# Third product of mixer 1 as a fourth inner seven-product, joined operand sums, and fillers spread over four inner products

## The chip, the cores and the metric

The kernel runs on one core of one Trainium2 chip. The metric is the time of one execution on the device in microseconds (us). The 35 executions of the kernel before agree within 0.2% (566.54 to 567.64 us), and kernels are compared only with the runs of the kernel before that were taken on the same chip in the same call, several rounds each. The results also list the mean clock that TensorE was granted in each run, with 1.0 as full speed.

Five engines appear below. TensorE (PE) multiplies matrices, and its weight loads (PEld) overlap the multiplications (in the kernel before they are busy 296.6 us and the multiplications 558.1, in a span of 566.0). VectorE (DVE) adds and subtracts. ScalarE (ACT) copies and applies gelu. SP and GpSimd play no part in the argument.

## The reference

The reference is one block of linear attention followed by a "mixer" MLP that works across the sequence. Only the first product of the mixer matters here.

```python
x = A_x                                             # 1 x 2048 x 1024, bf16
h = x + _A_ref(_layernorm(x, axis=-1), A_wqkv, A_wo)    # _A_ref is cut: linear attention, 32 heads
# _B_ref(_layernorm(h), w1, b1, w2, b2):
h = _layernorm(x, axis=-1)
u = jnp.einsum("bsd,sf->bdf", h, w1) + b1           # w1: 2048 x 3584: "mixer 1"
u = _gelu(u)
y = jnp.einsum("bdf,fs->bds", u, w2) + b2           # w2: 3584 x 2048: "mixer 2"
# cut: the result is h before the second layernorm, plus y transposed
```

## The kernel before

The kernel computes mixer 1 with a product of 2x2 blocks that needs seven multiplications instead of eight (of the Strassen-Winograd kind). A `Product7` object is one row block of the result. Its seven products are `p1` to `p7`; the products 5, 6, 7 and 3 need a left operand that is a sum of blocks, made by `asum` on VectorE. Two such objects make a `Quad`. Mixer 1 is seven quads: quad 0 is special, and quads 1 to 6 ("steady quads") all run through `run1`.

Inside a quad, some products of the two row blocks together are done once more by a seven-product, an `Inner`. It replaces 2 x 8 matmuls of 512 columns by 7 x 4 matmuls of 256 columns, and it pays with sums on VectorE and copies on ScalarE. The kernel before does this for product 1 (`in1`), product 5 (`in5`) and product 2 (`in2`). Product 3 is still sixteen plain matmuls (`sts[0].p3()`, `sts[1].p3_mm()`).

```python
class Inner:
    # ... (cut: __init__)
    def sums(self):                       # four operand sums on VectorE
        sm = [pools["is"].tile([P, self.nk, P], FP16, tag=self.tag, bufs=pools["is_bufs"], name="is")[:] for _ in range(4)]
        dve.tensor_tensor(sm[0], self.a21, self.a22, ALU.add)
        dve.tensor_tensor(sm[1], sm[0], self.a11, ALU.subtract)
        dve.tensor_tensor(sm[2], self.a11, self.a21, ALU.subtract)
        dve.tensor_tensor(sm[3], self.a12, sm[1], ALU.subtract)
        self.lhs.update({5: sm[0], 6: sm[1], 7: sm[2], 3: sm[3]})
    # ... (cut: mm, four matmuls of 256 columns)
    def i1(self):
        # ... (cut: takes the PSUM banks a, b, c, e)
        self.mm(1, self.a, True)
        nc.scalar.copy(self.b, self.a)    # L254: product 6 adds into this copy
    def i6(self):
        self.mm(6, self.b, False)
        nc.scalar.copy(self.c, self.b)    # L258
    # ... (cut: i2, i5)
    def i7(self):
        self.mm(7, self.c, False)
        self.sink_sum(1, 1, self.c, self.es[:])
    def i3(self):
        self.mm(3, self.b, False)
        self.sink_sum(0, 1, self.b, self.es[:])
    def i4(self):
        self.mm(4, self.c, False)
        self.sink(1, 0, self.c)           # what takes the result out of the bank
```

The steps of an inner product depend on each other through copies and adds. `interleave` therefore puts "fillers" between them, matmuls of 512 columns of other products that TensorE can do meanwhile. The names in quotation marks are points at which other work is put into the program.

```python
def interleave(self, n, fs, at={}):
    steps = [(f, k) for f in fs for k in range(self.sts[0].nk)]
    t = len(steps)
    cuts = [0, (5 * t + 8) // 16, (9 * t + 8) // 16, (12 * t + 8) // 16, t]
    # ... (cut)
    for f in (
        n.i1, "in", 0, n.i6, n.i2, 1, n.i5, n.i7, flush, 2, "mid", n.i3, "third", 3, n.i4, "out", flush,
    ):      # 0 to 3: the next share of the fillers
        # ... (cut)

def sink1(self, m, h, ps):                # result of in1: into A, and a copy into B
    A, B, c = self.sts[m].A, self.sts[m].B, self.cols(h)
    nc.scalar.copy(A[:, c], ps)
    nc.scalar.copy(B[:, c], A[:, c])

def sum1(self, m, h, ps, es):             # the same where a sum is due
    A, B, c = self.sts[m].A, self.sts[m].B, self.cols(h)
    dve.tensor_tensor(A[:, c], ps, es, ALU.add)
    nc.scalar.copy(B[:, c], A[:, c])

def run1(self, pend, nxt, on_p4):
    sts = self.sts
    def starting():
        self.asums(5)
        self.in5 = Inner(sts, 5, self.mov5, "i5", self.sink5, self.sum5)
        self.in5.sums()
        pend[1].p3_evac()
        for st in sts:
            st.begin(based=True)

    self.interleave(
        self.in1, [st.p4 for st in pend], {"in": starting, "mid": partial(sts[0].asum, 6)}
    )
    sts[1].asum(6)
    self.asums(7)
    in2 = Inner2(sts, 2, self.mov2, "i1", self.sink2, None)
    in2.sums()
    # ... (cut)
    self.interleave(self.in5, [st.p6 for st in sts])
    sts[0].finish()
    self.asums(3)
    self.interleave(in2, [st.p7_fill for st in sts], {
        "third": lambda: sts[0].evac(0, 0, sts[0].A), "out": lambda: sts[1].evac(0, 0, sts[1].A),
    })
    if nxt is not None:
        nxt.begin1()
    sts[0].p3()
    sts[1].p3_mm()
    return sts, nxt
```

Matmuls and the VectorE work of `dve` are pinned in mixer 1: they run in the order of the program.

## Time and profile before

| | kernel before |
|---|---|
| median of 3 runs | 566.69 us (566.56 to 567.57) |
| span of the profiled run | 566.0 us |
| PE / DVE / ACT busy | 99% / 73% / 49% |
| granted clock | 1.0 |
| the six steady quads | 23.22 us the first, then 22.98 or 22.99 |

The page of the profile starts with the busy time of each engine. Further down stands the chain of work that ended last, by engine; "issue" is time in which the engine waited for nothing that the profile shows, and a q behind a name (below, SPq) is the engine's sequencer. These lines are from the page of the kernel before.

```profile
span 566.0 us, 8365 instructions
...
PE 558.1 (99%) x3127; PEld 296.6 (52%) x3143; DVE 411.3 (73%) x798; ACT 277.4 (49%) x585; POOL 1.8 (0%) x8
...
PE 96%; DVE 2%; ACT 1%; issue 1%; DMA 0%
```

TensorE is busy almost all the time, and the granted clock of this run is 1.0. So a change gains where it takes matmul time away without opening a gap, and VectorE has time to spare only as long as its results come when TensorE asks for them.

The next view is the table of stretches for the first and the third steady quad of the kernel before, one quad to a row. In the kernel before the rows start 0.60 us behind the first matmul of the quad's first inner product (255.79 and 302.00), where the modelled end of product 1 stands. After the length come the busy time and the number of instructions of each engine, the granted clock, and the transfers.

```profile
core 0: us, PE busy (x) PEld busy (x) DVE busy (x) ACT busy (x) POOL busy (x), PEclk, DMA share, GB/s
256.39:279.61 23.22, 23.21 (x149) 14.46 (x148) 18.20 (x40) 11.77 (x26) 0.00 (x0) 1.00 0.29 92
302.60:325.58 22.98, 22.98 (x149) 14.48 (x148) 16.22 (x37) 11.75 (x26) 0.00 (x0) 1.00 0.30 93
```

The third quad has 22.98 us of PE work in 22.98 us. VectorE works 16.2 us in a quad and ScalarE 11.75.

The place is the start of the second inner product, `in5`. Here is TensorE's order in time, from the kernel before. The columns are start and length in us, then engine, line and operation, the output and the inputs with their sizes, and a count of equal instructions in a row.

```profile
308.51 0.60 PE L216 MATMUL psI<-hE,sa 128*128 128x256 f16 x4
308.94 1.24 PE L216 MATMUL psB<-hT,sa 128*128 128x512 f16 x5
310.02 0.60 PE L216 MATMUL psI<-hi,is 128*128 128x256 f16 x4
```

Product 1 of `in5` starts at 308.51, five fillers at 308.94, product 6 at 310.02. Five fillers at 0.2158 us each end exactly at 310.02, so there is no gap. The lengths shown overlap: each 512-column matmul is listed with 0.379 us although the next starts after 0.2158. (The notes of the profile page call the ends of matmuls modelled.) I therefore measure gaps between start times: a gap is the next start minus the last start minus the issue spacing.

Product 6 needs ScalarE's copy of product 1. This is ScalarE in order of time at the same place; a bracket gives the idle time before an instruction and what ended it.

```profile
308.38 0.38 ACT L495 COPY psB<-a 128x256 f32<-128x256 f32 x1 [0.61 <-DVE a L216]
308.70 0.68 ACT L419 ACTIVATE gO<-psC,b_sb 128x512 f16<-128x512 f32 x1
309.28 0.36 ACT L489 COPY a<-psI 128x256 f32<-128x256 f32 x1
309.53 0.39 ACT L254 COPY psI<-psI 128x256 f32<-128x256 f32 x1
```

The copy at line 254 is the one. It starts at 309.53 and ends at 309.92, 0.10 us before product 6. Before it ScalarE does a copy that waits for a VectorE add, a gelu, and a copy out of PSUM. They ran in that order: the copy starts at 308.38, after 0.61 us in which ScalarE idled for the add, and the gelu behind it at 308.70, although the last matmuls into the `psC` that it reads are listed from 307.21 to 308.24.

### The profile page before, as it was taken

To read this page: it belongs to the slowest core of one execution; us is meant where nothing else is said; L and a number is where in the kernel's file an instruction comes from. 1 tells how busy PE (TensorE), PEld (TensorE's weight loads), DVE (VectorE), ACT (ScalarE), POOL (GpSimd) and SP (SyncE) were. 2 spreads that over 40 slices of the span, in tenths; PEclk is the share of its full clock that TensorE was granted. 3 is DMA by queue.
4 is the path that set the end of the run, shared out by engine and by line. 5 is a ranking of instruction groups with operands and counts; after the bars stand their busy time and mean duration, and the time that the engine had idled before them with its cause. 6 is when DMAs were issued, how large, how long until landed. Compare 5 with 4: busy or idle time off the path is not lost.

```text
span 566.0 us, 8365 instructions
## 1 busy us (share of the span) xinstructions
PE 558.1 (99%) x3127; PEld 296.6 (52%) x3143; DVE 411.3 (73%) x798; ACT 277.4 (49%) x585; POOL 1.8 (0%) x8
## 2 busy tenths in 40 slices
PE   7999999999999999999999999999999999999997
PEld 3444444454444444456666666665445655645643
DVE  6898888544776788878768676676979749658725
ACT  4647777766766877645446454464210311311211
POOL 1000000000000000000000000000000000000000
PEclk9999999999999999999999999999999999999999
DMA  9933342115764751104041340422983922912111
GB/s 300 295 75 75 75 89 43 19 39 200 217 198 137 254 185 74 74 1 129 23 148 35 116 148 2 149 78 53 242 222 95 264 71 75 293 43 75 38 47 46
DMA packets 86088, 67.13 MB, mean 119 GB/s; under 512 B 15762, under 2 KB 80032, under 8 KB 86048
## 3 DMA queue, kind: packets, MB, share of 16 engines
q1 hardware_dynamic: 85312, 65.94, 40.6%
q10 hardware_dynamic: 672, 0.66, 0.3%
q8 instruction: 24, 0.39, 0.3%
q14 instruction: 16, 0.13, 0.1%
q0 software_dynamic: 64, 0.01, 0.0%
HBM read 54.54 MB, written 8.91 MB: 112 GB/s over the span
## 4 chain that ended last, share of the span: by engine, by line
PE 96%; DVE 2%; ACT 1%; issue 1%; DMA 0%
PE acc_t L216 18%; PE psI L216 16%; PE psC L216 15%; PE psB L216 15%; PE psA L216 4%; PE psC L814 4%; PE psB L814 4%; PE psA L814 4%; PE acc_t L738 3%; PE psA L325 2%; PE psB L325 2%; PE acc_t L1089 2%; PE psE L814 2%; PE psC L325 2%; PE kvps L767 1%; PE psE L325 1%
## 5 line engine op out<-in xcount | busy, mean ns | idle before, releaser
L216 PEld LDWEIGHTS <-sa 128*128 128x128 f16 x651 | 63.7, 98 | 48.5 <-issue 0.2
L216 PEld LDWEIGHTS <-wq 128*128 128x128 bf16 (+1 forms) x629 | 61.1, 98 | 46.8
L216 PEld LDWEIGHTS <-is 128*128 128x128 f16 x472 | 46.1, 98 | 21.6 <-DVE hi L216 0.4
L216 PE MATMUL acc_t<-wo_sb,pqT 128*128 128x512 f16 x256 | 55.6, 379 | 0.0
L216 PE MATMUL psC<-gs,wq 128*128 128x512 f16 (+2 forms) x210 | 45.0, 365 | 0.0
L216 PE MATMUL acc_t<-xnT,wq_sb 128*128 128x512 bf16 x188 | 43.1, 379 | 0.2
L216 PEld LDWEIGHTS <-pqT 128*128 128x128 bf16 x256 | 25.0, 98 | 30.5 <-issue 0.6
L178 DVE TENSOR_SCALAR e_sb<-e_sb 128x512 bf16<-128x512 bf16 x64 | 18.6, 290 | 27.9 <-ACT e_sb L174 27.3
L174 ACT ACTIVATE e_sb<-acc_t 128x512 bf16<-128x512 f32 x40 | 23.9, 597 | 24.6 <-PE acc_t L216 12.0
L814 PEld LDWEIGHTS <-xs 128*128 128x128 f16 x208 | 20.0, 98 | 23.4 <-DVE xs L800 1.3
L216 DVE TENSOR_TENSOR ot<-ot,hr 128x512 bf16<-128x512 bf16 (+2 forms) x27 | 11.2, 414 | 28.1 <-ACT ot L466 27.7
L216 PEld LDWEIGHTS <-wq_sb 128*128 128x128 bf16 x192 | 18.5, 98 | 23.0 <-issue 1.3
L362 ACT COPY psC<-psB 128x512 f32<-128x512 f32 x22 | 12.5, 570 | 34.6 <-PE psB L216 29.9
L216 PE MATMUL psB<-hT,sa 128*128 128x512 f16 x112 | 28.7, 379 | 0.0
L216 PE MATMUL psC<-hT,sa 128*128 128x512 f16 x112 | 28.3, 379 | 0.0
L216 DVE BATCH_NORM_STATS2 hst<-acc_t 128x6 f32<-128x512 f32 x32 | 21.4, 692 | 9.1 <-ACT h_bf L216 8.9
L216 DVE TENSOR_TENSOR a<-psI,a 128x256 f32<-128x256 f32 x36 | 14.7, 422 | 17.9 <-PE psI L216 17.2
L254 ACT COPY psI<-psI 128x256 f32<-128x256 f32 x25 | 9.1, 364 | 37.7 <-PE psI L216 37.4
L814 PE MATMUL psA<-wkv,xnT 128*128 128x512 bf16 x98 | 26.0, 379 | 0.3
L216 PE MATMUL psB<-hO,sa 128*128 128x512 f16 x112 | 25.3, 379 | 0.0
L814 PEld LDWEIGHTS <-xnT 128*128 128x128 bf16 x156 | 15.2, 98 | 18.5 <-issue 0.2
L258 ACT COPY psI<-psI 128x256 f32<-128x256 f32 x25 | 8.9, 357 | 32.3 <-PE psI L216 32.3
(202 smaller groups left out, 1046.2 us busy)
## 6 DMA issues: line engine op xcount, KB each, us to landing
wq<-in_B_w_dram SPq DMA_DIRECT2D x14, 1024.0 KB, 7.9
wq<-in_B_w_dram SPq DMA_DIRECT2D x8, 1792.0 KB, 9.2
xr<-in_A_x_dram SPq DMA_DIRECT2D x16, 256.0 KB, 4.7
rdb<-rd_dram SPq DMA_DIRECT2D x32, 128.0 KB, 4.0
h_dram<-h_bf SPq DMA_DIRECT2D x16, 256.0 KB, 2.0
hr<-h_dram SPq DMA_DIRECT2D x32, 128.0 KB, 2.6
out_dram<-ot SPq DMA_DIRECT2D x31, 128.0 KB, 1.7
x_sb<-in_A_x_dram SPq DMA_DIRECT2D x15, 256.0 KB, 3.0
```

Of the source, the lines that this page charges most:

```text
L174: pin(nc.scalar.activation(e_sb[:], src, ACT.Exp))
L178: pin(nc.vector.tensor_scalar(e_sb[:], e_sb[:], 1.0, PHI_EPS, ALU.min, ALU.add))
L216: return (lambda *a, **kw: pin(op(*a, **kw))) if self.always or Held.on else op
L254: nc.scalar.copy(self.b, self.a)
L258: nc.scalar.copy(self.c, self.b)
L325: pe.matmul(ps[:, cols], lhsT=lhs[:, k, :], rhs=mv(k)[:, cols], start=(start and k == 0), stop=(k == self.nk - 1), skip_group_check=True,)
L362: nc.scalar.copy(self.C[:], self.B[:])
L738: mm = nc.tensor.matmul(pp[:, 0:CW], lhsT=xnT[:, kt, i * P:(i + 1) * P], rhs=wkv[:, kt, c * CW:(c + 1) * CW], start=(kt == 0), stop=(kt == ...
L767: pin(nc.tensor.matmul(kv_ps[b][:, sl, :], lhsT=pks[i % NPK][:, j * P:(j + 1) * P], rhs=vaugs[i % NVA][:, j, :], start=False, stop=(i == N ...
L814: pin(nc.tensor.matmul(ps[:], lhsT=lhs[:, k, :], rhs=rhs[:, k, :], start=(start and k == 0), stop=(k == hk2 - 1), skip_group_check=True,))
L1089: nc.tensor.matmul(qp[:, 0:SW], lhsT=wq_sb[:, kt, j * P:(j + 1) * P], rhs=xnT[:, kt, u * SW:(u + 1) * SW], start=(kt == 0), stop=(kt == ND ...
```

## The change

The change has four parts.

1. Product 3 becomes a fourth inner seven-product, `in3`. That is 28 matmuls of 256 columns instead of 16 of 512. Its moving operand, the right half of `hO` (the last quarter of `h`), needs four 1024-wide sums (`sums3`, into the tile `hi`), once, in the first steady quad.
2. The operand sums of the two row blocks are made in one instruction of twice the width.
3. The fillers are spread over four inner products: 16, 12, 12 and 8 matmuls instead of 16, 16 and 16.
4. The sums of an inner product may be made in two parts, so that they can be placed separately.

The core of the diff, with cuts marked:

```diff
@@ Inner
-        def sums(self):
-            # ... four instructions
+        def sums(self, part=slice(0, 4)):
+            # ... the same four instructions, those in `part`
@@ Quad
         def asums(self, m):
-            for st in self.sts:
-                st.asum(m)
+            # ... (cut: Mixer2 as before; a, b are now views over both row blocks)
+            t = self.S[m] = pools["sa"].tile([P, NSP, 2, P], FP16, tag="sa", name="sa")[:]
+            for s, st in enumerate(self.sts):
+                st.lhs[m] = t[:, :, s, :]
+            return dve.tensor_tensor(t, a, b, op)
@@ run1
-        def run1(self, pend, nxt, on_p4):
+        def run1(self, pend, nxt, on_p4, before_third=nop):
             sts = self.sts
+            s4, s6, s7 = self.steps(*[st.p4 for st in pend]), self.steps(*[st.p6 for st in sts]), self.steps(*[st.p7_fill for st in sts])
+            c6, c7 = 3 * len(s6) // 4, len(s7) // 2
             def starting():
+                self.in1.sums(slice(2, 4))
                 self.asums(5)
                 self.in5 = Inner(sts, 5, self.mov5, "i5", self.sink5, self.sum5)
-                self.in5.sums()
-                pend[1].p3_evac()
-                # ...
+                self.in5.sums(slice(0, 2))
+                self.asums(6)
+                # ...
-            self.interleave(
-                self.in1, [st.p4 for st in pend], {"in": starting, "mid": partial(sts[0].asum, 6)}
-            )
-            sts[1].asum(6)
+            self.interleave(self.in1, s4, {"in": starting, "mid": lambda: self.in5.sums(slice(2, 4))})
             self.asums(7)
             # ...
-            self.interleave(self.in5, [st.p6 for st in sts])
+            self.interleave(self.in5, s6[:c6])
             sts[0].finish()
             self.asums(3)
-            self.interleave(in2, [st.p7_fill for st in sts], {
+            self.base3()
+            in3 = Inner2(sts, 3, self.mov3, "i5", self.add_to(self.t3), None)
+            in3.sums()
+            before_third()
+            sts[0].with_shared(sts[0].base3, sts[0].B)
+            self.interleave(in2, s6[c6:] + s7[:c7], {
                 # ...
-            sts[0].p3()
-            sts[1].p3_mm()
+            self.interleave(in3, s7[c7:], {
+                "third": lambda: sts[0].evac(0, 1, sts[0].base3), "out": lambda: sts[1].evac(0, 1, sts[1].base3),
+            })
@@ main
+    mov3, sums3 = inner_moving(hO[:, :, CW:D], NSP, inner1, "hi3")
-        pend, nxt = cur.run1(pend, lambda: ..., next_load1(u + 1))
+        pend, nxt = cur.run1(pend, lambda: ..., next_load1(u + 1), sums3 if u == 1 else nop)
```

The result of product 5 in `Inner2` is added to both row blocks by one broadcast instruction, and intermediate sums are written in place.

More of the change, by code (lines that the diff above doesn't have):

```diff
@@ L2 @@
 from functools import partial
+from itertools import groupby
 import concourse.bass as bass
@@ L229, in __init__ @@
             self.lhs = {1: self.a11, 2: self.a12, 4: self.a22}
-        def sums(self):
-            sm = [pools["is"].tile([P, self.nk, P], FP16, tag=self.tag, bufs=pools["is_bufs"], name="is")[:] for _ in range(4)]
-            dve.tensor_tensor(sm[0], self.a21, self.a22, ALU.add)
-            dve.tensor_tensor(sm[1], sm[0], self.a11, ALU.subtract)
-            dve.tensor_tensor(sm[2], self.a11, self.a21, ALU.subtract)
-            dve.tensor_tensor(sm[3], self.a12, sm[1], ALU.subtract)
-            self.lhs.update({5: sm[0], 6: sm[1], 7: sm[2], 3: sm[3]})
+        def sums(self, part=slice(0, 4)):
+            if part.start == 0:
+                self.sm = [pools[self.tag].tile([P, self.nk, P], FP16, tag=self.tag, bufs=pools["is_bufs"], name="is")[:] for _ in range(4)]
+                self.lhs.update(zip((5, 6, 7, 3), self.sm))
+            sm = self.sm
+            for o, a, b, op in (
+                (sm[0], self.a21, self.a22, ALU.add), (sm[1], sm[0], self.a11, ALU.subtract),
+                (sm[2], self.a11, self.a21, ALU.subtract), (sm[3], self.a12, sm[1], ALU.subtract),
+            )[part]:
+                dve.tensor_tensor(o, a, b, op)
         def mm(self, m, ps, start):
@@ L283, in i5 @@
             self.mm(5, self.e, True)
-            for m in range(2):
-                self.sink(m, 1, self.e)
+            self.sink(slice(0, 2), 1, self.e)
         def i7(self):
@@ L335, in whole, with begin @@
             return ks is None or ks[-1] == self.nk - 1
-        def begin(self, based=False):
-            if based:
-                self.A = pools["t"].tile([P, BANK], F32, tag=f"a{self.p % 2}", name="a1")
-            else:
-                self.A = psw.tile([P, BANK], F32, tag="w", name="psA1")
+        def begin(self, A=None):
+            self.A = psw.tile([P, BANK], F32, tag="w", name="psA1") if A is None else A
             self.B = psx.tile([P, BANK], F32, tag="x", name="psB1")
@@ L422, in evac, with with_shared @@
             )
+        def with_shared(self, t, ps):
+            dve.tensor_tensor(t, ps[:], self.e[:], ALU.add)
         def evac_shared(self, fh, ps):
-            t = pools["t"].tile([P, BANK], F32, tag=f"t{fh}", name="t1")
-            dve.tensor_tensor(t[:], ps[:], self.e[:], ALU.add)
+            t = self.base3 if fh == self.apart else self.e
+            self.with_shared(t[:], ps)
             self.evac(fh, 1, t)
@@ L479, with __init__ @@
     class Quad:
-        def __init__(self, sts, mov1=None, mov5=None, mov2=None):
+        def __init__(self, sts, mov1=None, mov5=None, mov2=None, mov3=None):
             self.sts = sts
-            self.mov1, self.mov5, self.mov2 = mov1, mov5, mov2
+            self.mov1, self.mov5, self.mov2, self.mov3 = mov1, mov5, mov2, mov3
+            self.S = {}
         def cols(self, h):
@@ L501, in sum5, with steps, interleave @@
             dve.tensor_tensor(self.sts[m].e[:, self.cols(h)], ps, es, ALU.add)
-        def interleave(self, n, fs, at={}):
-            steps = [(f, k) for f in fs for k in range(self.sts[0].nk)]
+        def steps(self, *fs):
+            return [(f, k) for f in fs for k in range(self.sts[0].nk)]
+        def interleave(self, n, steps, at={}):
             t = len(steps)
@@ L510, in fill @@
             def fill(q):
-                part = steps[cuts[q]:cuts[q + 1]]
-                for f in fs:
-                    ks = [k for g, k in part if g is f]
-                    if ks:
-                        f(ks, late)
+                for f, part in groupby(steps[cuts[q]:cuts[q + 1]], lambda s: s[0]):
+                    f([k for _, k in part], late)
             def flush():
@@ L529, in asums @@
         def asums(self, m):
-            for st in self.sts:
-                st.asum(m)
+            if not isinstance(self.sts[0], Mixer1):
+                for st in self.sts:
+                    st.asum(m)
+                return
+            v = w1_tiles[self.sts[0].p // 2].rearrange("p (k two) (s h f) -> p k two s h f", two=2, s=2, h=2)
+            a11, a12, a21, a22 = (v[:, :, k, :, h, :] for h in range(2) for k in range(2))
+            a, b, op = {
+                5: (a21, a22, ALU.add),
+                6: (self.S.get(5), a11, ALU.subtract),
+                7: (a11, a21, ALU.subtract),
+                3: (a12, self.S.get(6), ALU.subtract),
+            }[m]
+            t = self.S[m] = pools["sa"].tile([P, NSP, 2, P], FP16, tag="sa", name="sa")[:]
+            for s, st in enumerate(self.sts):
+                st.lhs[m] = t[:, :, s, :]
+            return dve.tensor_tensor(t, a, b, op)
         def inner(self, m):
@@ L550, in run2 @@
             self.asums(6)
-            self.interleave(self.in1, [st.p4 for st in pend])
+            self.interleave(self.in1, self.steps(*[st.p4 for st in pend]))
             on_p4()
@@ L559, in run2 @@
             self.asums(7)
-            self.interleave(in5, [st.p6 for st in sts])
+            self.interleave(in5, self.steps(*[st.p6 for st in sts]))
             self.asums(3)
@@ L574, in run2, with run_first @@
             return sts, nxt
-        def run_first(self, nxt, before_inner):
+        def run_first(self, nxt, before_inner, before_second):
             sts = self.sts
@@ L584, in run_first @@
             self.in5.mov = self.mov5
-            self.interleave(self.in5, [st.p6 for st in sts])
+            self.interleave(self.in5, self.steps(*[st.p6 for st in sts]))
             before_inner(slice(2, 4))
             nxt.begin1()
+            self.base3()
+            for i, st in enumerate(sts):
+                st.apart = 1
+                st.p7()
+                before_second(slice(2 * i, 2 * i + 2))
             for st in sts:
-                st.p7()
-            sts[0].p3()
-            sts[1].p3_mm()
+                st.p3()
@@ L592, in run_first, with base, base3 @@
             return sts, nxt
+        def base(self, tag):
+            return pools["t"].tile([P, 2, BANK], F32, tag=tag, name=tag)
+        def base3(self):
+            self.t3 = self.base("t3")
+            for s, st in enumerate(self.sts):
+                st.base3, st.apart = self.t3[:, s, :], 0
         def begin1(self):
             self.in1 = Inner(self.sts, 1, self.mov1, "i1", self.sink1, self.sum1)
-            self.in1.sums()
-        def sink2(self, m, h, ps):
-            t = self.sts[m].A[:, self.cols(h)]
-            dve.tensor_tensor(t, ps, t, ALU.add)
@@ L602, in run1, with add_to, sink @@
-        def run1(self, pend, nxt, on_p4):
+            self.in1.sums(slice(0, 2))
+        def add_to(self, base):
+            def sink(m, h, ps):
+                c = self.cols(h)
+                if isinstance(m, slice):
+                    ps = ps.unsqueeze(1).to_broadcast([P, 2, HW])
+                dve.tensor_tensor(base[:, m, c], ps, base[:, m, c], ALU.add)
+            return sink
+        def run1(self, pend, nxt, on_p4, before_third=nop):
             sts = self.sts
+            s4, s6, s7 = self.steps(*[st.p4 for st in pend]), self.steps(*[st.p6 for st in sts]), self.steps(*[st.p7_fill for st in sts])
+            c6, c7 = 3 * len(s6) // 4, len(s7) // 2
@@ L605, in starting @@
             def starting():
+                self.in1.sums(slice(2, 4))
                 self.asums(5)
                 self.in5 = Inner(sts, 5, self.mov5, "i5", self.sink5, self.sum5)
-                self.in5.sums()
-                pend[1].p3_evac()
-                for st in sts:
-                    st.begin(based=True)
-            self.interleave(
-                self.in1, [st.p4 for st in pend], {"in": starting, "mid": partial(sts[0].asum, 6)}
-            )
-            sts[1].asum(6)
+                self.in5.sums(slice(0, 2))
@@ L617, in run1 @@
+                self.asums(6)
+                self.t1 = self.base("t1a")
+                for s, st in enumerate(sts):
+                    st.begin(self.t1[:, s, :])
+            self.interleave(self.in1, s4, {"in": starting, "mid": lambda: self.in5.sums(slice(2, 4))})
             self.asums(7)
-            in2 = Inner2(sts, 2, self.mov2, "i1", self.sink2, None)
+            in2 = Inner2(sts, 2, self.mov2, "i1", self.add_to(self.t1), None)
             in2.sums()
@@ L623, in run1 @@
                 st.shared_tile()
-            self.interleave(self.in5, [st.p6 for st in sts])
+            self.interleave(self.in5, s6[:c6])
             sts[0].finish()
             self.asums(3)
-            self.interleave(in2, [st.p7_fill for st in sts], {
+            self.base3()
+            in3 = Inner2(sts, 3, self.mov3, "i5", self.add_to(self.t3), None)
[3 more added lines that the diff above has]
+            self.interleave(in2, s6[c6:] + s7[:c7], {
                 "third": lambda: sts[0].evac(0, 0, sts[0].A), "out": lambda: sts[1].evac(0, 0, sts[1].A),
             })
+            sts[1].with_shared(sts[1].base3, sts[1].B)
             if nxt is not None:
                 nxt.begin1()
-            sts[0].p3()
-            sts[1].p3_mm()
+            self.interleave(in3, s7[c7:], {
+                "third": lambda: sts[0].evac(0, 1, sts[0].base3), "out": lambda: sts[1].evac(0, 1, sts[1].base3),
+            })
             return sts, nxt
@@ L1175 @@
         wpool = sactx.enter_context(tc.tile_pool(name="wpool", bufs=2, side="right"))
-        pools["sa"] = mctx.enter_context(tc.tile_pool(name="sapool1", bufs=8, side="right"))
+        pools["sa"] = mctx.enter_context(tc.tile_pool(name="sapool1", bufs=4, side="right"))
         def load_wo(c):
             nc.sync.dma_start(wo_sb[:, :, c * CW:(c + 1) * CW], wo_v[:, :, c * CW:(c + 1) * CW])
-        pools["is"] = mctx.enter_context(tc.tile_pool(name="is0", bufs=1, side="right"))
+        pools["i5"] = mctx.enter_context(tc.tile_pool(name="is0", bufs=1, side="right"))
         pools["is_bufs"] = 4
@@ L1321, in first_sums @@
                 for m in (5, 6, 7, 3):
-                    for st in cur.sts:
-                        yield pin(st.asum(m))
+                    yield pin(cur.asums(m))
                 cur.in5 = Inner(cur.sts, 5, None, "i5", cur.sink5, cur.sum5)
@@ L1328, in first_sums @@
                 yield cur
-            sums_at, ahead = (11, 12, 13, 14, 17, 18, 19, 20, 21), first_sums()
+            sums_at, ahead = (11, 13, 17, 19, 21), first_sums()
             scale_at = {7: (0, 0), 8: (0, 1), 15: (1, 0), 16: (1, 1), 23: (2, 0)}
@@ L1401 @@
     inner1 = mctx.enter_context(tc.tile_pool(name="inner1", bufs=1, side="right"))
-    pools["is"], pools["is_bufs"] = inner1, 4
+    pools["i1"] = inner1
     hmov.update(moving(hE, hO, hT2, hT3, hT4))
@@ L1418, in quad1 @@
     def quad1(u):
-        return Quad([Mixer1(2 * u), Mixer1(2 * u + 1)], mov1, mov5, mov2)
+        return Quad([Mixer1(2 * u), Mixer1(2 * u + 1)], mov1, mov5, mov2, mov3)
     Held.on = True
@@ L1423 @@
     cur.mov5 = mov5
-    pend, nxt = cur.run_first(quad1(1), sums1)
-    sums2()
+    pend, nxt = cur.run_first(quad1(1), sums1, sums2)
     for u in range(1, NQ1):
         cur = nxt
-        pend, nxt = cur.run1(pend, lambda: quad1(u + 1) if u + 1 < NQ1 else None, next_load1(u + 1))
+        pend, nxt = cur.run1(pend, lambda: quad1(u + 1) if u + 1 < NQ1 else None, next_load1(u + 1), sums3 if u == 1 else nop)
     Held.on = False
-    pend[1].p3_evac()
     for st in pend:
@@ L1440 @@
     inner2 = ctx.enter_context(tc.tile_pool(name="inner2", bufs=1, side="right", reuse_waits="tile"))
-    pools["is"], pools["is_bufs"] = inner2, 7
+    pools["i"], pools["is_bufs"] = inner2, 7
     H2 = NFP // 2
```

## The prediction

> **What bounds the kernel now.** TensorE. The page's first part has PE busy 558.1 of 566.0 us (99%), and the chain of waits is 96% PE at a granted clock of 1.0. In mixer 1 the timeline shows six quads back to back. The middle ones take 22.98 us each without a PE gap; the stretches table gives VectorE 16.2 us and ScalarE 11.75 us per quad. Matmuls issue every 0.2158 us (512 columns) and 0.1086 us (256 columns). [...]
>
> **What the change does, per quad (six of them).**
> - PE: 16 matmuls of 512 columns (3.45 us) become 28 of 256 (3.04 us): 0.41 us less, 2.5 us over six quads.
> - VectorE: the eight operand sums (0.60 us apart) become four of twice the width. The trace has a 2048-wide sum at 1.22 us, so this saves only about 0.3 us. New: four inner sums (0.34 to 0.46 each) and five adds out of PSUM (0.34, one 0.60): about 3.3 us. Net about +3 us, to about 19.3 of 22.6.
> - ScalarE: two more copies, +0.6 us.
> - Once, in the first steady quad: four 1024-wide sums of h's last quarter, 0.72 us apart, 2.8 us of VectorE. They stand in VectorE's order right before the adds of the third inner product.
> - Fillers (512-column matmuls that cover the copies between inner products) drop from 16 to 12, 12 and 8 in three of the inner products.
>
> **How much is on the critical path.** The 0.41 us is wholly on PE. But [...] the cover is thinner. I laid the measured durations end to end in the new orders:
> 1. In the second inner product, four fillers instead of five stand before product 6. Before, its PSUM copy landed at about 309.92 us for a matmul at 310.02: nearly no slack. VectorE also reaches the last sum of the first product about 0.2 us later. I expect a PE gap of about 0.3 us per quad there.
> 2. In the first steady quad the 2.8 us of sums delay the adds of the third inner product. Its product 4 needs a PSUM bank that one of them reads; slack about 0.15 to 0.3 us, so a single PE gap of about 2.5 us.
> 3. Other slots (fourth inner product, products 6 and 4) have 0 to 0.2 us to spare.
>
> Sum: steady quads 22.98 to about 22.86 (five times, -0.6), first quad 23.22 to about 25.2 (+2.0). Elsewhere 0: the order of mixer 2 and the attention hardly changes.
>
> **Prediction: 567.8 us**, range 565.2 to 569.3. Faster by over 2%: 0.01; within 2%: 0.98; slower by over 2%: 0.01.
>
> **What would show it.** Right: one gap of 2 to 3 us in PE in the first steady quad, waiting for VectorE adds; quads of 22.8 to 22.9 us with a gap of 0.2 to 0.4 us at product 6 of the second inner product, waiting for a ScalarE copy; VectorE about 19 us per quad. Wrong: no PE gaps and quads of 22.5 us, then the time is near 564.2.
>
> **What would make it wrong.** Shorter VectorE hand-offs than I laid out (all gaps close: 564 to 565); or further slots with no slack opening 0.1 to 0.3 us gaps each per quad (569 to 570).

The laying end to end assumed that VectorE and ScalarE keep the order they are given. The traces below fit it at the places shown (the 0.61 us above, the two gaps of 2.60 and 0.28 us below).

## More of the kernel before

The ScalarE copies are not pinned, and the scheduler of the build places them.

## The result, and the profile after

| | before | after |
|---|---|---|
| median, same chip | 566.83 us (566.56 to 567.57, 4 runs) | 569.0 us (568.27 to 570.28, 4 runs) |
| ratio after / before | | 1.0039, 95% interval 1.0015 to 1.0063 |
| span of the profiled run | 566.0 us | 567.9 us |
| mixer 1, first steady quad to the first matmul of mixer 2 | 141.59 us | 143.29 us |
| mixer 2, start of its first matmul to start of its last | 165.03 us | 165.03 us |
| first steady quad | 23.22 us | 25.54 us |
| other steady quads | 22.98 us | 22.86 us |

A ratio is the mean time of one kernel's fast runs over that of the other's of the same rounds, so it is not quite the ratio of the medians quoted. At a threshold of 2% the kernel is the same. It is slower by about 0.4%. The four runs are 569.72, 568.27, 568.28 and 570.28 us; their mean granted clocks are 1.0, 1.0, 1.0 and 0.997. Keep the last one in mind. The first, which is the profiled one, is 1.4 us above the next two at the same clock: it reached the first steady quad at 256.04 us, where the repeat of the same kernel (below) did so at 254.95. So about a microsecond of it, and with it part of the median, comes from ahead of mixer 1 and not from the change. The stage times below are the better measure.

The same lines of the page, from the kernel after:

```profile
span 567.9 us, 8564 instructions
...
PE 557.9 (98%) x3215; PEld 303.8 (53%) x3215; DVE 431.6 (76%) x822; ACT 280.9 (49%) x597; POOL 1.8 (0%) x8
...
PE 85%; DVE 9%; ACT 2%; DMA 2%; issue 1%; SPq 1%; DVEq 0%; ACTq 0%
```

VectorE does 20 us more. The chain now goes over VectorE for 9%, but that share is not a cost: it shows where the chain passed, not what it lost there. (In the first experiment below it is still 7% in a run that is faster than the kernel before.) What was lost stands in the view of TensorE's waits. It lists the output waited with, the releaser, the total in us, the number of times and the longest. These lines are from the kernel after; the waits left out are of the start and of the attention stage.

```profile
PE psI L217 <- DVE t1a L217: 2.4, 1, 2.4
...
PE psI L217 <- ACT psI L258: 0.2, 1, 0.2
```

There is one long wait for a VectorE add in mixer 1; the short one, for ScalarE, is that at product 6 of `in5` in the first steady quad. In the kernel before, this view lists no wait of TensorE for an inner product (`psI`) at all. The stretches of the kernel after, columns as above:

```profile
256.04:281.58 25.54, 22.91 (x162) 15.64 (x160) 21.66 (x43) 11.75 (x28) 0.00 (x0) 1.00 0.26 83
281.58:304.44 22.86, 22.75 (x163) 15.65 (x161) 19.32 (x40) 12.28 (x29) 0.00 (x0) 1.00 0.29 93
304.44:327.30 22.86, 22.75 (x163) 15.64 (x161) 19.33 (x40) 12.28 (x29) 0.00 (x0) 1.00 0.29 92
```

The first steady quad became 2.32 us longer, each other one 0.12 us shorter. 2.32 - 5 x 0.12 = 1.7 us, which is the whole change of the stage.

**The long gap.** In the kernel before, product 4 of `in2` in the first steady quad follows its four fillers at once (274.26 + 4 x 0.2158 = 275.12):

```profile
274.26 1.03 PE L216 MATMUL psC<-hT,sa 128*128 128x512 f16 x4
275.12 0.60 PE L216 MATMUL psI<-hi,wq 128*128 128x256 f16 x4
```

TensorE at the same place of the kernel after:

```profile
273.11 0.81 PE L217 MATMUL psC<-hT,sa 128*128 128x512 f16 x3
276.36 0.60 PE L217 MATMUL psI<-hi,wq 128*128 128x256 f16 x4 [2.45 <-DVE t1a L217]
```

The three fillers from 273.11 take until 273.76 at 0.2158 us each; product 4 of `in2` starts at 276.36. That is a gap of 2.60 us. The bracket says 2.45 because it counts from the estimated end of the last filler. And this is what VectorE does meanwhile:

```profile
271.39 0.68 DVE L217 TENSOR_TENSOR hi<-hO 128x1024 f16<-128x1024 f16 x1
...
273.56 0.69 DVE L217 TENSOR_TENSOR hi<-hO,hi 128x1024 f16<-128x1024 f16 x1
274.17 0.68 DVE L217 TENSOR_TENSOR t<-psB,e 128x512 f32<-128x512 f32 x1
274.77 1.87 DVE L217 TENSOR_TENSOR t1a<-psI,t1a 128x256 f32<-128x256 f32 x4
```

The four sums of `hO` (`sums3`) run from 271.39 to 274.25. Behind them stand a 512-wide add and the adds to `t1a`, out of the banks that `in2` needs back. In this trace they start only behind the sums, at 274.17 and 274.77. That it was the place of the sums is tested in the first experiment: with them moved, the gap of 2.60 us is gone.

**The short gap.** TensorE at the start of `in5` in the second steady quad of the kernel after, and then ScalarE at the same place:

```profile
288.09 0.60 PE L217 MATMUL psI<-hE,sa 128*128 128x256 f16 x4
288.52 1.03 PE L217 MATMUL psB<-hT,sa 128*128 128x512 f16 x4
289.66 0.60 PE L217 MATMUL psI<-hi,is 128*128 128x256 f16 x4
```

```profile
288.08 0.38 ACT L499 COPY psB<-t1a 128x256 f32<-128x256 f32 x1 [0.68 <-DVE t1a L217]
288.39 0.68 ACT L419 ACTIVATE gO<-psC,b_sb 128x512 f16<-128x512 f32 x1
288.97 0.36 ACT L493 COPY t1a<-psI 128x256 f32<-128x256 f32 x1
289.23 0.39 ACT L258 COPY psI<-psI 128x256 f32<-128x256 f32 x1
```

Now four fillers start at 288.52. They take until 289.38, but product 6 starts at 289.66, a gap of 0.28 us. No wait view shows it at this place, because the estimated end of the last filler (289.55) covers most of it. Counted from the start of product 1, the copy that product 6 needs (here line 258) ends after 1.53 us, where before it was 1.41. So the copy comes 0.12 us later, the fillers end 0.22 us earlier (four instead of five), and 0.06 us of slack is used up: before, the copy ended 0.10 us ahead of product 6, and now product 6 follows it after 0.04. 0.12 + 0.22 - 0.06 = 0.28.

### The profile page after: what moved, and what is told of

It reads as the page before. It is cut to its first block, busy times and chain, and to the rows that moved or that the text cites. A ratio compares the mean times of both kernels' runs of the same rounds, so it can differ in the third digit from the quotient of the medians.

```text
span 567.9 us, 8564 instructions
## 1 busy us (share of the span) xinstructions
PE 557.9 (98%) x3215; PEld 303.8 (53%) x3215; DVE 431.6 (76%) x822; ACT 280.9 (49%) x597; POOL 1.8 (0%) x8
## 4 chain that ended last, share of the span: by engine, by line
PE 85%; DVE 9%; ACT 2%; DMA 2%; issue 1%; SPq 1%; DVEq 0%; ACTq 0%
PE acc_t L217 18%; PE psI L217 15%; PE psC L217 11%; PE psB L217 10%; PE psA L217 4%; PE psB L854 4%; PE psC L854 4%; PE psA L854 4%; DVE is L217 3%; PE acc_t L1129 2%; PE psB L328 2%; PE psA L328 2%; PE psE L854 2%; DVE sa L217 2%; PE psC L328 2%; DMA x_sb<-in_A_x_dram 2%
## 5 line engine op out<-in xcount | busy, mean ns | idle before, releaser
L217 PEld LDWEIGHTS <-sa 128*128 128x128 f16 x627 | 61.3, 98 | 35.9
L217 PEld LDWEIGHTS <-is 128*128 128x128 f16 x568 | 55.5, 98 | 27.6 <-issue 2.4
L217 PE MATMUL psC<-hT,sa 128*128 128x512 f16 x112 | 31.2, 379 | 0.0
L217 PE MATMUL psI<-hi,is 128*128 128x256 f16 x200 | 30.0, 272 | 0.8 <-ACT psI L258 0.2
L258 ACT COPY psI<-psI 128x256 f32<-128x256 f32 x31 | 11.2, 362 | 38.8 <-PE psI L217 38.0
L217 PE MATMUL psC<-hT,wq 128*128 128x512 f16 x96 | 24.6, 379 | 0.0
L217 ACT CAST h_bf<-acc_t 128x512 bf16<-128x512 f32 x32 | 18.4, 581 | 12.0 <-PE acc_t L217 12.0
```

The costliest lines, as they stand in the source:

```text
L217: return (lambda *a, **kw: pin(op(*a, **kw))) if self.always or Held.on else op
```

## The experiments

The theory, from the traces: without its two gaps the change is about 2.6 us faster than the kernel before; the long gap is caused by where the four sums stand in VectorE's order; the short gap is caused by fewer fillers and by the order of adds and copies around `in5`. (No run gives the fifth filler back alone, so the filler's share, 0.22 us in the sum above, rests on that sum.) Three rivals were possible. The joined 2048-wide sums could be too coarse for VectorE's order. The filler split could be wrong. Or the new adds out of PSUM could simply be too much for VectorE. All ten experiments gave correct results. A repeat of the change came first.

### The change once more

No edit.

> The changed kernel itself, run again on the chip of the three others, so that they can be compared with it. Both theories: about 2 us slower than the kernel before (ratio about 1.003 to 1.004), one PE gap of about 2.5 us in the first steady quad, 0.28 us per quad ahead of product 6 of the second inner product, steady quads of 22.86 us.

Measured: 568.56 us (568.32 to 570.31, 6 runs) against 566.76 of the kernel before on that chip; ratio 1.0035 (1.0023 to 1.0047). The runs are in two groups: four of 568.32 to 568.72 at clock 1.0, and two of 570.19 and 570.31 at clock 0.997. The profile fell in the second group. This is its table of stretches around the long gap, in slices of 1 us; the third number from the end is the granted clock.

```profile
274.00:275.00 1.00, 0.00 (x0) 0.00 (x0) 0.90 (x3) 0.00 (x0) 0.00 (x0) 1.00 0.00 0
275.00:276.00 1.00, 0.72 (x4) 0.52 (x4) 0.56 (x2) 0.41 (x1) 0.00 (x0) 0.57 0.02 8
...
278.00:279.00 1.00, 1.00 (x7) 0.66 (x6) 0.71 (x2) 0.79 (x2) 0.00 (x0) 0.73 0.00 0
279.00:280.00 1.00, 1.00 (x9) 0.71 (x8) 0.42 (x1) 0.36 (x1) 0.00 (x0) 1.00 0.00 0
```

About the end of the gap (TensorE resumes at 275.28) the clock goes to one half for some microseconds, 3.41 us from finer slices (275.14 to 278.55). The bracketed wait in front of it is 2.45 us, as in the first profile, where the clock did not fall. In this run mixer 1 took 144.89 us, 1.60 more than in the profile at full clock. So the change has a second cost that the first profile doesn't show: in two of these six executions the mean clock is 0.997, and in the profiled one of them it fell to one half at the end of the gap.

### The sums of hO moved into idle time of VectorE

```diff
@@ run1, on the change
             in2.sums()
+            before_third()
             ...
             in3.sums()
-            before_third()
@@ main, on the change
+    def before_inner(part):
+        sums1(part)
+        if part.start == 0:
+            sums3(slice(0, 1))
-    pend, nxt = cur.run_first(quad1(1), sums1, sums2)
+    pend, nxt = cur.run_first(quad1(1), before_inner, sums2)
-        ..., next_load1(u + 1), sums3 if u == 1 else nop)
+        ..., next_load1(u + 1), partial(sums3, slice(1, 4)) if u == 1 else nop)
```

The first sum goes into quad 0, the other three behind the sums for `in2`, in the first steady quad. The work is the same.

> Only the place of the four sums of h's last quarter differs: the first one goes into an idle stretch of VectorE in the quad before, the other three into the 2.1 us that VectorE idles during the second inner product of the first steady quad. Theory: the one gap of 2.45 us in PE is made by where these sums stand, so it closes entirely; the first quad falls from 25.54 to about 22.9 to 23.1 us and the time by 2.4 us against the change, to about 0.3 us below the kernel before; the 0.28 us gap per quad stays. Rival (VectorE is too full in this quad wherever the sums stand, since it does 21.7 us of work in 25.5): the gap only moves or shrinks to 1 us or more, and the time falls by less than 1.5 us.

Measured: 566.38 us (565.79 to 566.5, 5 runs); ratio to before 0.9989 (0.9977 to 1.0001). All five runs at clock 1.0. TensorE at the place of the long gap, in this run:

```profile
271.81 0.81 PE L217 MATMUL psC<-hT,sa 128*128 128x512 f16 x3
272.45 0.60 PE L217 MATMUL psI<-hi,wq 128*128 128x256 f16 x4
```

The three fillers end at 272.46 and product 4 starts at 272.45. The gap is gone. The first steady quad is 22.94 us, the others are still 22.86, and mixer 1 takes 140.69 us, 2.60 less than in the change. This hit the expectation. VectorE was busy as long as in the change, in each later quad (19.33 us) and in the whole (431.5 against 431.6 us). In the first steady quad it did 0.67 us less, the sum that went to quad 0, which is too little for a gap of 2.60. So it was mainly the place and not the amount.

### The second pair of sums for in5 placed later

```diff
@@ run1, on the change
-            self.interleave(self.in1, s4, {"in": starting, "mid": lambda: self.in5.sums(slice(2, 4))})
+            self.interleave(self.in1, s4, {"in": starting, "third": lambda: self.in5.sums(slice(2, 4))})
```

The two sums of `in5` now stand behind the add of `in1`'s product 3, whose result ScalarE copies first at the start of `in5`.

> Only the last two sums for the second inner product are issued after, not before, the add that takes product 3 of the first inner product out of PSUM. Theory: the per-quad gap is made by that add coming 0.6 us late in VectorE's order, which holds up four ScalarE instructions in a row; the gap of 0.28 us closes, steady quads take 22.52 to 22.6 us, and the time falls by 1.5 to 1.9 us against the change; the gap of 2.45 us stays. Rival (the gap comes from having four filler matmuls in place of five ahead of product 6): the add's place does not matter, quads stay at 22.86 us within 0.05.

Measured: 569.61 us (569.23 to 570.17, 5 runs); ratio 1.005 (1.0038 to 1.0062). Two things happened. The steady quads became 22.73 us, so half of the short gap closed; 22.5 to 22.6 was expected, and that was missed. And all five runs were at clock 0.997, which hides the gain in the whole time: the long gap was left in, 2.62 us between issue slots, and the clock fell every time. Against the two runs of the change at that clock (570.19 and 570.31) it is 0.6 to 0.7 us less, which agrees with five times 0.13.

### Both

Both edits together.

> Both edits together. Theory: no PE gap over 0.1 us is left in mixer 1, all steady quads take 22.5 to 22.6 us, and the whole matmul saving of 0.41 us per quad shows: about 4.0 us below the change and 2.0 to 2.6 us below the kernel before (ratio about 0.996). Rival (28 short matmuls of 256 columns do not really run in less time than 16 of 512, because each needs its weights loaded): no gap, but quads near 22.9 us, and a time equal to the kernel before within 0.5 us.

Measured: 565.45 us (564.87 to 565.83, 5 runs); ratio 0.9974 (0.9962 to 0.9986). The quads are 22.73 us and mixer 1 takes 139.84. Against the kernel before it is 1.31 us less by the medians, where 2.0 to 2.6 were expected: missed, and for one reason. Here are TensorE and then ScalarE of this run at the start of `in5`:

```profile
307.47 1.03 PE L217 MATMUL psB<-hT,sa 128*128 128x512 f16 x4
308.48 0.60 PE L217 MATMUL psI<-hi,is 128*128 128x256 f16 x4
```

```profile
307.38 0.36 ACT L493 COPY t1a<-psI 128x256 f32<-128x256 f32 x1
307.78 0.38 ACT L494 COPY psB<-t1a 128x256 f32<-128x256 f32 x1
308.09 0.34 ACT L258 COPY psI<-psI 128x256 f32<-128x256 f32 x1
```

The copy that waits for the add comes early now (at 306.45, where product 1 starts at 307.03; in the change, 288.08 against 288.09). But the scheduler used the freed time to put the copy to `psB` at line 494 ahead of the copy that product 6 needs. That one ends at 308.43, product 6 starts at 308.48, and the fillers had ended at 308.33: a gap of 0.15 us.

### Both, with that copy held back

```diff
@@ Inner.i1, on the kernel with both edits
-            nc.scalar.copy(self.b, self.a)
+            (hs if self.hold else nc.scalar).copy(self.b, self.a)   # hs: ScalarE, pinned
@@ Quad.sink1
-            nc.scalar.copy(B[:, c], A[:, c])
+            if m == 1 and isinstance(self.sts[0], Mixer1):
+                self.late_copy = lambda: hs.copy(B[:, c], A[:, c])
+            else:
+                nc.scalar.copy(B[:, c], A[:, c])
@@ run1
-            self.interleave(self.in5, s6[:c6])
+            self.in5.hold = True
+            self.interleave(self.in5, s6[:c6], {"in": self.late_copy})
```

> As e3_both, with one ScalarE copy held back: in e3_both the scheduler had put the copy of the last quarter of B ahead of the copy that product 6 of the second inner product waits for, which leaves a gap of 0.15 us per quad (quads of 22.73 us). Here that copy is held behind it. Theory (ScalarE's order made the rest of the gap): quads of 22.55 to 22.62 us, no PE gap over 0.05 us in steady quads, 0.7 to 1.0 us below e3_both, so about 564.6 us and 2.1 us below the kernel before. Rival (four fillers are too few whatever the order): quads stay at 22.7 us or more.

Measured: 564.42 us (564.15 to 564.93, 5 runs) against 567.07 on that chip; ratio 0.9955 (0.9942 to 0.9967). This is the best version, 2.65 us below the kernel before. The steady quads are 22.59 us, mixer 1 takes 138.97, and no gap above 0.03 us between matmuls is left in them. ScalarE's copies in the order wanted, from this run:

```profile
306.83 0.36 ACT L493 COPY t1a<-psI 128x256 f32<-128x256 f32 x1
307.12 0.36 ACT L217 COPY psI<-psI 128x256 f32<-128x256 f32 x1
307.38 0.38 ACT L217 COPY psB<-t1a 128x256 f32<-128x256 f32 x1
```

The copy that product 6 needs ends at 307.48, and product 6 starts at 307.78, right when its fillers end:

```profile
306.92 1.03 PE L217 MATMUL psB<-hT,sa 128*128 128x512 f16 x4
307.78 0.60 PE L217 MATMUL psI<-hi,is 128*128 128x256 f16 x4
```

The expectation was hit for the quads and the gap; the whole gained a little more than the 2.1 us expected. The quads now differ from those of the kernel before by 22.98 - 22.59 = 0.39 us, and the arithmetic of the matmuls says 16 x 0.2158 - 28 x 0.1092 = 0.40. (The prediction's 0.1086 us for 256 columns was read a little low: the traces have 109 or 110 ns from start to start, 109.2 on average, so its 0.41 should have been 0.40.) So the whole of the PE saving is there once the gaps are closed, and the rival "too many adds for VectorE" falls: VectorE's busy time is nearly the same as in the change (19.42 against 19.32 us in a quad).

### The operand sums apart again

On the kernel with the sums of `hO` moved:

```diff
@@ Quad.asums
-            return dve.tensor_tensor(t, a, b, op)
+            for s in range(2):
+                ins = hv.tensor_tensor(t[:, :, s, :], a[:, :, s, :], b[:, :, s, :], op)
+            return ins
```

> e1_sums_early with the operand sums of the two pairs in two instructions again, each half as wide. Durations laid end to end: VectorE has 0.06 to 0.1 us more per sum, the scheduler swaps one gelu and one copy on ScalarE, the PE gap moves from product 6 (0.28) to the first filler of the second inner product (0.35): quads of 22.88 to 22.95 us against 22.86, the first quad 0.2 to 0.4 us longer, 0.3 to 0.9 us above e1_sums_early in all. Rival (joining the sums was what made room for the fourth inner product): 2 us or more above e1_sums_early. Other rival (joining is worth nothing): within 0.2 us of e1_sums_early.

Measured: 566.32 us (566.21 to 567.18, 5 runs); ratio to before 0.9989 (0.9976 to 1.0003), the same ratio as with the sums joined, from another call. The quads are 22.92 us instead of 22.86, as expected, the first one is 0.13 us longer (0.2 to 0.4 was expected), and mixer 1 is 0.45 us longer. The gap moved to the first filler of `in5`, because the scheduler also swapped the gelu and a copy. So joining the sums is worth about 0.06 us a quad together with what it does to that order. The whole time doesn't resolve it. The rival that the joined sums are harmful is refuted for the quads, where they help a little.

### More fillers in in5

On the best version, all sixteen `p6` matmuls as fillers of `in5`, and so eight for `in2`:

```diff
-            c6, c7 = 3 * len(s6) // 4, len(s7) // 2
+            c6, c7 = len(s6), len(s7) // 2
```

> e6_copy_held with the fillers as before the change in the second inner product: all 16 of product 6 there, so 8 and 8 are left for the third and fourth. Theory (VectorE stands 0.2 to 0.3 us ahead of product 4 of the third inner product, and four fillers fewer are 0.86 us less cover): a PE gap of 0.4 to 0.5 us per quad at that product, waiting for VectorE, quads of 22.95 to 23.05 us, 2.3 to 2.8 us above e6_copy_held. Rival (once the sums are moved the spread of fillers does not matter): within 0.3 us of e6_copy_held.

Measured: 567.21 us (566.94 to 567.82, 5 runs); ratio 1.0004 (0.9991 to 1.0016), 2.79 us above the best version. The quads are 23.07 us. Two fillers instead of three stand before product 4 of `in2`, and in every quad it starts 0.48 us late, after a VectorE add to `t1a`. The gap and the time hit the expectation; the quads are just above its 22.95 to 23.05. The split 12 and 12 is not the fault of the change; taking fillers from `in2` would have been worse.

### The long gap made longer

On the change, the first of the four sums is made three times:

```diff
-        ..., sums3 if u == 1 else nop)
+        ..., (lambda: (sums3(slice(0, 1)), sums3(slice(0, 1)), sums3())) if u == 1 else nop)
```

> The changed kernel with the first of the four sums of h's last quarter done three times (same values), so 1.2 to 1.4 us more VectorE work at the spot of the one long gap. Theory of the clock (a PE gap of about 2.5 us makes the granted clock fall to half for about 3 us in some executions, at 1.6 us each; a longer gap does it every time): the gap is 3.6 to 3.9 us, every execution shows a clock below 1.0, and the time is about 571.3 us, without the two groups of runs that the change has (568.3 and 570.3). Rival (the two groups of runs have another cause, with no tie to the gap): still two groups, 1.3 us higher each, and executions at clock 1.0 among them.

Measured: 571.62 us (571.46 to 571.66, 4 runs); ratio 1.008 (1.0067 to 1.0094). All four runs at clock 0.997. The gap is 4.06 us between issue slots (3.90 in the wait view, in which 3.6 to 3.9 was expected), and mixer 1 takes 146.43. A hit. The stretches of this run, columns as above:

```profile
275.00:276.00 1.00, 0.00 (x0) 0.00 (x0) 1.00 (x3) 0.00 (x0) 0.00 (x0) 1.00 0.00 0
276.00:277.00 1.00, 0.41 (x4) 0.37 (x4) 0.82 (x3) 0.04 (x1) 0.00 (x0) 1.00 0.00 0
277.00:278.00 1.00, 1.00 (x8) 0.60 (x7) 0.77 (x2) 1.00 (x3) 0.00 (x0) 0.88 0.03 8
278.00:279.00 1.00, 1.00 (x5) 0.59 (x4) 1.00 (x3) 1.00 (x3) 0.00 (x0) 0.50 0.00 0
```

TensorE starts again at 276.59, and at first its clock is still full. It falls at 277.76, 1.2 us after the gap has ended, and stays at one half for 3.41 us.

### Half of the long gap

Two of the four sums are moved as in the first experiment and two left:

```diff
@@ on the kernel with the sums moved
+            before_second()        # sums3(slice(1, 2)), behind in2.sums()
             ...
+            before_third()         # sums3(slice(2, 4)), behind in3.sums()
```

> The changed kernel with two of the four sums of h's last quarter moved to the places of e1_sums_early and two left where they stood, so that the long gap shrinks to 1.0 to 1.2 us. Theory of the clock: a gap of that length never makes the granted clock fall, so every execution shows clock 1.0 (0.999 at least), one group of runs, about 566.7 to 567.1 us. Rival (any gap there can do it): executions at 0.997 among them, 1.6 us above the rest.

Measured: 567.47 us (567.2 to 567.72, 5 runs) against 566.84; ratio 1.0009 (0.9997 to 1.0021). The gap is 1.15 us, and all five runs are at clock 1.0, as expected. The time is 0.4 us above the expected range: a miss. Mixer 1 takes 141.81 us, 1.12 more than the 140.69 of the version without the gap, which is the gap. By the medians, too, the version without the gap stood 0.38 us below the kernel before and this one stands 0.63 above it, 1.0 apart. So the gap cost its own length and nothing more, and the expected range was drawn too low.

### A gap of 3.3 us

On the change, the first sum is made twice:

```diff
-        ..., sums3 if u == 1 else nop)
+        ..., (lambda: (sums3(slice(0, 1)), sums3())) if u == 1 else nop)
```

> The changed kernel with the first of the four sums done twice, so that the gap is 3.1 to 3.3 us, between those of the change (2.45, clock fell in 3 of 10 executions) and e7_long_gap (3.9, fell in all). If the length of the gap decides, the clock falls in most or all executions: 570.8 to 571.0 us where it falls, 569.0 to 569.2 where it does not. If it is the place of the gap in time and not its length, the share stays near 3 in 10.

Measured: 569.98 us (569.06 to 571.56, 6 runs); ratio 1.0055 (1.004 to 1.007). The gap is 3.33 us. Three of six runs are at clock 0.997 (570.66 to 571.56), three at 1.0 (569.06 to 569.31). "Most or all" was too strong.

### What the runs say of the clock

| gap between issue slots | kernel | runs at clock 0.997 |
|---|---|---|
| none above 0.5 us | five experiments without the long gap | 0 of 25 |
| 1.15 us | half of the long gap | 0 of 5 |
| 2.6 us | the change | 3 of 10 |
| 2.6 us | second pair of sums later | 5 of 5 |
| 3.3 us | first sum twice | 3 of 6 |
| 4.1 us | first sum three times | 4 of 4 |

In all four kept traces that hold a fall the granted clock goes from 1.0 to 0.5, stays there for 3.41 us (worked out from slices of 0.2 us) and goes back to 1.0. Where the fall begins differs:

| run | TensorE resumes | clock falls |
|---|---|---|
| first sum twice | 276.08 | 275.32, 0.76 us before |
| the change, repeated | 275.28 | 275.14, 0.14 us before |
| second pair of sums later | 275.23 | 275.42, 0.19 us after |
| first sum three times | 276.59 | 277.76, 1.2 us after |

In the first profile of the change the gap was 2.60 us and the clock stayed at 1.0.

So the mean clock was 0.997 in none of the 30 runs of the table with gaps up to 1.15 us, and in 15 of its 25 with gaps of 2.6 us or more. The share does not simply grow with the length: one kernel with 2.6 us had the lower clock in five runs of five, another in three of ten, and the one with 3.3 us in three of six. What decides between the two kinds of runs of one kernel is not shown, and no experiment set a gap between 1.15 and 2.6 us.

## Why the prediction was right or wrong

The prediction said 567.8 us and "same", with 565.2 to 569.3 as the range. The median was 569.0, inside the range, at its upper end. Point by point:

- **TensorE bounds the kernel, and product 3 saves 0.41 us a quad.** Right, but for the 0.01 us of the low reading told above. With all gaps closed the quads are 0.39 us shorter, and the whole is 2.65 us faster.
- **A gap of about 0.3 us at product 6 of the second inner product, in every quad.** Right: 0.28. Both named causes fit the traces (fewer fillers, and VectorE reaching the add later; 0.12 us, where 0.2 was predicted); the place of the add was tested, the filler alone was not. The steady quads came out at 22.86, the number predicted. The experiments add that two orders had to be mended to close it, VectorE's and ScalarE's: the first alone gave half.
- **One gap of about 2.5 us in the first steady quad from the four sums.** Right in place, cause and size: 2.60. Moving the same sums away closed it.
- **First steady quad about 25.2 us.** Too low by 0.34: it was 25.54. With 22.59 for a quad without gaps, 22.59 + 2.60 + 0.35 = 25.54, where the 0.35 is the gap at product 6 in this quad. The prediction's own terms were too small here, and the step "first quad 23.22 to about 25.2 (+2.0)" should have been +2.3.
- **Sum.** The terms written down give +2.0 - 0.6 = +1.4, that is about 568.1 from 566.69; the prediction says 567.8 and does not say where the other 0.3 went. Measured in the stage at full clock: +1.70.
- **VectorE about 19.3 us and ScalarE +0.6 us a quad; elsewhere no change.** Right: 19.32 and +0.53 us; the matmuls of mixer 2 span 165.03 us in both.
- **The joined sums save about 0.3 us of VectorE a quad.** Right: with the sums apart VectorE is busy 19.60 us in a quad, with them joined 19.33. The 2048-wide sum cost what was assumed, 1.22 us. That the saving moves the time by only about 0.06 us a quad fits VectorE not being the bound.
- **Missed: the clock.** The prediction treated a gap as costing its own length. In three of ten executions of the change the mean clock was 0.997; in the one of them that was profiled it fell to one half at the end of the gap, for 3.41 us, which cost about 1.6 us more. Those runs (570.19 to 570.31) lie above the range. The first call's median of 569.0 mixes two ordinary runs of 568.3 with one at the lower clock and one that lost a microsecond ahead of mixer 1, so where it falls in the range is partly chance; the stage, +1.70 against +1.4, says more of the prediction.

So the intended gain of about 2.5 us was real. It went to a single queue of four VectorE sums, to a 0.28 us gap in each of the other quads, and in some runs to the slower clock.

## What to carry to other kernels

When work is moved from the bounding engine to one with spare time, lay out the order around each hand-off: here the same VectorE work cost 2.6 us in one place and nothing in another. If removing a gap brings less than expected, look at what the scheduler put into the time you freed. And if a change leaves TensorE idle in one place, look at the clocks of several runs, because one profile may show only the cheaper kind: here gaps of 2.6 us and more came with a mean clock of 0.997 in 15 of 25 runs, and one of 1.15 us in none of five.
